# Loading x as plain partition quarters and turning it on VectorE, in place of DMA transposes, in a dense-Mish-dense kernel

## The chip, the cores and the metric

The kernel runs on one core of a Trainium2 chip. The metric is device time in microseconds of one execution; smaller is better. Engines: TensorE (matmuls, with weight loads listed apart as PEld), VectorE (DVE), ScalarE (ACT), GpSimd (POOL) and SyncE (SP). Two engines issue the DMAs here, SP and ACT; each has a queue of its own.

## The reference

```python
B, S, D, F = 1, 2048, 512, 1792          # all bf16
h   = jnp.einsum("bsd,df->bsf", x, w1) + b1
sp  = jnp.log1p(jnp.exp(-jnp.abs(h))) + jnp.where(h > 0, h, 0)
act = h * jnp.tanh(sp)                   # Mish
out = jnp.einsum("bsf,fd->bsd", act, w2)
```

Two dense layers with a Mish between them: 2048 tokens, 512 inputs, 1792 hidden units, 512 outputs.

## The kernel before

The program is written by hand, with one instruction stream for each engine and semaphores between them. Each stream counts its own finished work, and `wait` puts a wait into a stream only where that count isn't known to be reached yet. `load` issues a DMA and gives it a semaphore of its own.

**Layouts.** The first product contracts over D = 512, which is four K tiles of 128 on the partitions. So it needs x with D on the partitions: `xT[p, k, token]`. `w1_sb[p, k, f]` holds w1 with the same split of D. The product comes out as h with 128 hidden units on the partitions and 512 tokens in one PSUM bank (`mm1_step`); ScalarE adds b1 and applies Mish into `a_sb` (`mish`); the second product (`mm2`) contracts over the 14 hidden tiles and gives 128 tokens by 512 outputs, which VectorE copies to `o_sb` and SP stores (`put`).

**Blocks.** The tokens are worked in four blocks of 512. For each block: 14 hidden tiles f, each with four matmuls over K and one Mish; then four token tiles, each with 14 matmuls. Hidden tiles 0 to 3 of block 0 use PSUM banks 0 to 3; all others of the first product use bank 4 + f % 4, so f = 8 waits until the Mish of f = 4 has emptied bank 4. The second product uses banks 0 to 3.

**How x gets transposed.** A token tile is 128 tokens. Tiles 0 and 1 are loaded as they are into `x_nat` and transposed by TensorE against an identity, four pieces of 128x128 each, into PSUM, from where VectorE copies them to `xT` (`transpose_x`). Tiles 2 and 3 come by one DMA transpose straight into `xT`, and so do the blocks 1, 2 and 3, with one DMA transpose each (`load_xT`).

**The start.** Two ordered queues carry the loads. ACT: w1 for f 0 to 3 in two halves (K tiles 0 and 1, then 2 and 3), then b1, then the load of the activation table. SP: x tiles 0 and 1, the DMA transpose of tiles 2 and 3, w1 for f 4 to 7, w1 for f 8 to 13, w2 in two parts, then the DMA transposes of blocks 1 to 3. TensorE first runs ten dummy matmuls on constants (`WARM`, `GAP`), with the transposes of tile 0 between them. Then it works on f 0 to 3 of block 0 in the order in which x comes in: K tiles 0 and 1 on tile 0 (with tile 1's transposes in between), K tiles 0 and 1 on tile 1, K tiles 2 and 3 on both, and last all four K tiles on tiles 2 and 3, one f after the other, each followed by its Mish:

```python
for f in range(F0):
    for k in range(KT):
        mm = mm1_step(0, f, k, f, 2, 4)
    mish(0, f, f, pe.mark(mm))
```

b1 is loaded in 14 rows, copied into a zeroed 32x128 tile, turned by four 32x32 VectorE transposes and cast to float32 (`b1_sb`); every Mish needs it.

Of the kernel before, what the change touches and what calls it, by code (L numbers as in the profile page):

```python
# [4 lines left out]

P = 128
WARM = (512,) * 5 + (128,) * 3
GAP = (128,) * 2
FIRST = ((0, 2), (2, 4))
BLOCKS = (512, 512, 512, 512)  # L10


# [21 lines left out]
def bass_standalone__dense_activation_mish__prompt_kernel(  # L34
# [22 lines left out]
    with ExitStack() as es:  # L57
        def sb(name, shape, t):
            return es.enter_context(nc.sbuf_tensor(name, shape, t))

        x_nat = sb("x_nat", [P, 2, D], BF)
        xT = sb("xT", [P, KT, S], BF)
        w1_sb = sb("w1_sb", [P, KT, F], BF)
        w2_sb = sb("w2_sb", [P, FT, D], BF)
        b1_nat = sb("b1_nat", [FT, P], BF)
# [18 lines left out]
        def load(q, dst, src, name, transpose=False):  # L84
            s = sem(name)
            (q.eng.dma_start_transpose if transpose else q.eng.dma_start)(dst, src).then_inc(s, 16)  # L86
            return (s, 16)

        t_xn, t_w1, t_w2, t_xT = [None] * 2, {}, {}, {}

        def load_x(j):
            t_xn[j] = load(sp, x_nat[:, j, :], x2[j * P:(j + 1) * P, :], "s_xn%d" % j)
# [12 lines left out]
        def load_xT(lo, hi):  # L105
            t = load(sp, xT[:, :, lo:hi], x2[lo:hi, :], "s_xT%d" % lo, True)
            for j in range(lo // P, hi // P):
                t_xT[j] = t

        for ks in FIRST:  # L110
            load_w1(act, slice(*ks), 0, F0)
        load_x(0)
        load_x(1)
        t_b1 = load(act, b1_nat[:, :], b1.rearrange("(j p) -> j p", p=P), "s_b1")
        load_xT(2 * P, 4 * P)
        load_w1(sp, slice(0, KT), 4, 8)
        load_w1(sp, slice(0, KT), 8, FT)
        load_w2(0, 5)
        load_w2(5, FT)
        for s in range(1, len(BLOCKS)):  # L120
            load_xT(starts[s], starts[s + 1])

        t_bz = dve.mark(nc.vector.memset(b1_pad[:, :], 0.0))  # L123
# [9 lines left out]
        def dummy(n):  # L133
            nc.tensor.matmul(ps[:, 7, 0:n], c_w, c_m[:, 0:n], start=True, stop=True)  # L134

        free = [[] for _ in range(8)]
        t_cp = {}
        t_mish = {}


        def transpose_x(j, bank, ks):
            pe.wait(t_xn[j], t_id, *free[bank])
            psb = ps[:, bank, 0:2 * P].bitcast(BF)
            for i, k in enumerate(ks):
                mm = nc.tensor.transpose(psb[:, i * P:(i + 1) * P], x_nat[:, j, k * P:(k + 1) * P], ident[:, :])  # L145
            n = len(ks)
            dve.wait(pe.mark(mm))
            t = dve.mark(nc.vector.tensor_copy(xT[:, ks[0]:ks[0] + n, j * P:(j + 1) * P],  # L148
                                               psb[:, 0:n * P].rearrange("p (k t) -> p k t", k=n)))
            for k in ks:  # L150
                t_cp[j, k] = t
            free[bank] = [t]

        def mm1_step(s, f, k, bank, j0=0, j1=None):
            j1 = BLOCKS[s] // P if j1 is None else j1
            lo, hi = j0 * P, j1 * P
            first = k == 0 and j0 == 0
            if first:
                pe.wait(*free[bank])
            pe.wait(t_w1[k, f])  # L160
            for j in range(starts[s] // P + j0, starts[s] // P + j1):
                pe.wait(t_cp[j, k] if j < 2 else t_xT[j])
            return nc.tensor.matmul(ps[:, bank, lo:hi], w1_sb[:, k, f * P:(f + 1) * P],  # L163
                                    xT[:, k, starts[s] + lo:starts[s] + hi], start=first,
                                    stop=(k == KT - 1 and hi == BLOCKS[s]))

        def mish(s, f, bank, t_mm):
            act.wait(t_b1c, t_mm)
            t = act.mark(act.eng.activation(a_sb[:, f, starts[s]:starts[s + 1]], ps[:, bank, 0:BLOCKS[s]], ACT.Mish,  # L169
                                            bias=b1_sb[:, f:f + 1]))  # L170
            t_mish[s, f] = t
            free[bank] = [t]
# [13 lines left out]
        def mm2(i, lo, hi, bank, q=sp):  # L186
            s = max(b for b in range(len(BLOCKS)) if starts[b] <= i * P)
            pe.wait(*free[bank])
            for f in range(FT):
                pe.wait(t_w2[f], t_mish[s, f])  # L190
                mm = nc.tensor.matmul(ps[:, bank, 0:hi - lo], a_sb[:, f, i * P:(i + 1) * P], w2_sb[:, f, lo:hi],  # L191
                                      start=(f == 0), stop=(f == FT - 1))
# [9 lines left out]
        for k in range(2):  # L202
            for f in range(F0):
                mm1_step(0, f, k, f, 0, 1)
            if k == 0:
                transpose_x(1, 6, (0, 1))
                transpose_x(1, 4, (2, 3))
        dve.wait(t_b1, t_bz)
        t_b1p = dve.mark(nc.vector.tensor_copy(b1_pad[0:FT, :], b1_nat[:, :]))  # L209
        dve.wait(t_b1p)  # L210
        for c in range(P // 32):
            t_b1t = dve.mark(nc.vector.transpose(b1_t[c * 32:(c + 1) * 32, :], b1_pad[:, c * 32:(c + 1) * 32]))  # L212
        dve.wait(t_b1t)
        t_b1c = dve.mark(nc.vector.tensor_copy(b1_sb[:, :], b1_t[:, 0:FT]))  # L214
        for k in range(2):
            for f in range(F0):
                mm1_step(0, f, k, f, 1, 2)
        for k in range(2, KT):
            for f in range(F0):
                mm1_step(0, f, k, f, 0, 2)  # L220
        for f in range(F0):
            for k in range(KT):
                mm = mm1_step(0, f, k, f, 2, 4)
            mish(0, f, f, pe.mark(mm))
# [41 lines left out]
```

## Time and profile before

| | |
|---|---|
| median of three runs | 105.49 us (104.65, 105.49, 105.63) |
| profiled execution | 106.46 us, of which the span from first to last instruction is 105.2 us |
| TensorE busy | 101.3 us |
| ScalarE busy | 39.3 us |
| VectorE busy | 13.6 us |
| DMA | 7.94 MB in 13489 packets |

The profile shows one execution. Its times count from the start of the span. It lists, for each engine, groups of instructions by line of the kernel, operation and tile, with count, busy time and mean duration; the idle time ahead of a group with what ended it; the DMA issues with their time to landing; and the chain of work that ended last, followed back from the last instruction. Matmuls are pipelined and their ends are modelled, so their starts say more than their durations. All engine rows of `load` carry line 86, all matmuls of the first product line 163, of the second line 191; Mish is line 169, the copy of an output line 180.

### The profile page before, as it was taken

The page shows a single profiled execution, that of the slowest core. Times are in us where ns is not written, and L with a number is a line of the kernel's source. Part 1 is how long each engine was busy: PE and PEld are TensorE (multiplying, and loading weights), DVE is VectorE, ACT ScalarE, POOL GpSimd, SP SyncE. Part 2 cuts the span into 40 slices and gives each one's busy share as a digit, 9 for nine tenths or more (in the row PEclk, how much of TensorE's full clock was granted, in tenths as well). Part 3 has the DMA queues.
Part 4 walks back from the last instruction along what each step waited for, and adds up shares of the span by engine and source line. Part 5 has one row for each costly group of instructions (what it writes and reads, how often), then busy time and mean ns, then how long its engine had stood idle before and what let it go on. Part 6 is the DMA issues. An engine that isn't in the chain of part 4 may idle for free.

```text
span 105.2 us, 1142 instructions
## 1 busy us (share of the span) xinstructions
PE 101.3 (96%) x495; PEld 48.9 (47%) x504; DVE 13.6 (13%) x28; ACT 39.3 (37%) x57; POOL 0.7 (1%) x6
## 2 busy tenths in 40 slices
PE   6989999999999999999999999999999999999992
PEld 2667444444444444444444444444444444444462
DVE  0250000022220000022211000022112000011223
ACT  0406977200007777400006877600005777700000
POOL 2000000000000000000000000000000000000000
PEclk9999999999999999999999999999999999999999
DMA  2999999891111000001111000001111000001111
GB/s 40 319 109 361 355 349 275 170 229 44 50 50 50 0 0 6 0 0 50 50 50 50 0 0 0 3 6 50 50 50 50 0 0 0 0 0 53 53 50 50
DMA packets 13489, 7.94 MB, mean 76 GB/s; under 512 B 7852, under 2 KB 13484, under 8 KB 13484
## 3 DMA queue, kind: packets, MB, share of 16 engines
q1 hardware_dynamic: 12768, 7.31, 28.1%
q10 hardware_dynamic: 716, 0.56, 1.7%
q8 instruction: 4, 0.07, 0.3%
q14 instruction: 1, 0.01, 0.0%
HBM read 3.94 MB, written 2.10 MB: 57 GB/s over the span
## 4 chain that ended last, share of the span: by engine, by line
PE 90%; DMA 6%; SPq 1%; issue 1%; DVE 0%
PE ps L191 46%; PE ps L163 44%; DMA xT<-in_x_dram 6%; SPq L86 1%; DVE o_sb L180 0%
## 5 line engine op out<-in xcount | busy, mean ns | idle before, releaser
L169 ACT ACTIVATE a_sb<-ps,b_sb 128x512 bf16<-128x512 f32 x56 | 38.0, 688 | 50.0 <-PE ps L163 50.0
L163 PE MATMUL ps<-xT,w_sb 128*128 128x512 bf16 (+2 forms) x243 | 50.1, 365 | 0.9 <-DMA xT<-in_x_dram 0.6
L191 PE MATMUL ps<-w_sb,a_sb 128*128 128x512 bf16 (+2 forms) x234 | 48.8, 366 | 0.2
L163 PEld LDWEIGHTS ps<-xT,w_sb 128*128 128x128 bf16 x248 | 24.3, 101 | 25.7 <-DMA xT<-in_x_dram 0.9
L191 PEld LDWEIGHTS ps<-w_sb,a_sb 128*128 128x128 bf16 x238 | 22.8, 98 | 25.9
L180 DVE CAST o_sb<-ps 128x512 bf16<-128x512 f32 (+2 forms) x17 | 11.2, 660 | 84.4 <-PE ps L191 84.4
L134 PE MATMUL ps<-const-bfloat16-1.0 128*128 128x512 bf16 (+1 forms) x10 | 3.0, 467 | 0.8 <-PEq L251 0.8
L134 PEld LDWEIGHTS ps<-const-bfloat16-1.0 128*128 128x128 bf16 x10 | 1.2, 139 | 2.2 <-issue 2.2
L128 ACT ACT_TABLE_LOAD x1 | 1.3, 1283 | 2.6 <-issue 2.6
L148 DVE COPY xT<-ps 128x256 bf16<-128x256 bf16 (+2 forms) x4 | 1.1, 291 | 3.5 <-PE ps L145 3.4
L145 PE MATMUL ps<-ident,x_nat 128*128 128x128 bf16 x8 | 1.2, 310 | 0.0
L145 PEld LDWEIGHTS ps<-ident,x_nat 128*128 128x128 bf16 x8 | 0.7, 133 | 0.4 <-DMA x_nat<-in_x_dram 0.3
L212 DVE STREAM_TRANSPOSE b_t<-b_pad 32x32 bf16<-32x32 bf16 x4 | 0.8, 202 | 0.1
L209 DVE COPY b_pad<-b_nat 14x128 bf16<-14x128 bf16 x1 | 0.2, 182 | 1.1 <-DMA b_nat<-in_b_dram 1.1
L126 POOL TENSOR_SCALAR_AFFINE_SELECT ident<-ones 128x128 bf16<-128x128 bf16 x1 | 0.3, 295 | 0.1
L123 DVE MEMSET b_pad<- 32x64 uint32 x1 | 0.1, 112 | 0.9 <-PEq L251 0.9
L124 POOL MEMSET ones<- 128x128 bf16 x1 | 0.2, 205 | 0.3 <-POOLq L251 0.3
L214 DVE CAST b_sb<-b_t 128x14 f32<-128x14 bf16 x1 | 0.2, 175 | 0.0
L251 POOL MEMSET const-bfloat16-1.0<- 128x1 bf16 x1 | 0.1, 102 | 0.0
L251 POOL MEMSET const-uint8-127<- 128x1 uint8 x1 | 0.1, 102 | 0.0
L251 POOL MEMSET const-float32-0.0<- 128x1 f32 x1 | 0.1, 99 | 0.3 <-issue 0.3
L251 POOL MEMSET const-float32-1.0<- 128x1 f32 x1 | 0.1, 99 | 0.0
## 6 DMA issues: line engine op xcount, KB each, us to landing
out_dram<-o_sb SPq DMA_DIRECT2D x15, 128.0 KB, 1.7
w_sb<-in_w_dram SPq DMA_DIRECT2D x1, 1152.0 KB, 11.9
w_sb<-in_w_dram SPq DMA_DIRECT2D x1, 768.0 KB, 7.9
w_sb<-in_w_dram SPq DMA_DIRECT2D x1, 640.0 KB, 9.0
w_sb<-in_w_dram ACTq DMA_DIRECT2D x2, 256.0 KB, 3.8
w_sb<-in_w_dram SPq DMA_DIRECT2D x1, 512.0 KB, 6.4
x_nat<-in_x_dram SPq DMA_DIRECT2D x2, 128.0 KB, 3.0
out_dram<-o_sb SPq DMA_DIRECT2D x1, 96.0 KB, 1.6
```

Source lines behind the costliest of these rows:

```text
L86: (q.eng.dma_start_transpose if transpose else q.eng.dma_start)(dst, src).then_inc(s, 16)
L126: t_id = pool.mark(pool.eng.affine_select(ident[:, :], ones[:, :], pattern=[[1, P]], compare_op=ALU.is_equal, fill=0.0, base=0, channel_mu ...
L128: act.eng.preload_act_table(ACT.Mish)
L134: nc.tensor.matmul(ps[:, 7, 0:n], c_w, c_m[:, 0:n], start=True, stop=True)
L145: mm = nc.tensor.transpose(psb[:, i * P:(i + 1) * P], x_nat[:, j, k * P:(k + 1) * P], ident[:, :])
L148: t = dve.mark(nc.vector.tensor_copy(xT[:, ks[0]:ks[0] + n, j * P:(j + 1) * P], psb[:, 0:n * P].rearrange("p (k t) -> p k t", k=n)))
L163: return nc.tensor.matmul(ps[:, bank, lo:hi], w1_sb[:, k, f * P:(f + 1) * P], xT[:, k, starts[s] + lo:starts[s] + hi], start=first, stop=( ...
L169: t = act.mark(act.eng.activation(a_sb[:, f, starts[s]:starts[s + 1]], ps[:, bank, 0:BLOCKS[s]], ACT.Mish, bias=b1_sb[:, f:f + 1]))
L180: t = dve.mark(nc.vector.tensor_copy(o_sb[:, i, lo:hi], ps[:, bank, 0:hi - lo]))
L191: mm = nc.tensor.matmul(ps[:, bank, 0:hi - lo], a_sb[:, f, i * P:(i + 1) * P], w2_sb[:, f, lo:hi], start=(f == 0), stop=(f == FT - 1))
L212: t_b1t = dve.mark(nc.vector.transpose(b1_t[c * 32:(c + 1) * 32, :], b1_pad[:, c * 32:(c + 1) * 32]))
L251: nc = _bacc.Bacc("TRN2", target_bir_lowering=False, num_devices=1)
```

## The change

Three things change together.

*x.* Only tile 0 still goes through TensorE. Tiles 1 to 15 are loaded into `x_q` with plain DMAs, by quarters: a quarter a holds columns 128a to 128a + 127 of x, on the 32 partitions 32a to 32a + 31, with token t of a group of 32 tokens on partition 32a + t. Each run of a DMA is 128 elements, 256 bytes. VectorE then turns 32x32 pieces (`turn_x`): one instruction for each K tile, over all 128 partitions, reading every fourth element (a step of 8 bytes) and writing `xT`.

*w1.* Reading every fourth element means that partition p of K tile k holds row 4p + k of D, not row 128k + p. w1's rows are loaded in the same order (`"(p k) f -> p k f"`), and tile 0's transposes read `x_nat` with a step of four too.

*Order.* SP now issues x tile 0, two quarters of tile 1, the second half of w1 for f 0 to 3 (which was on ACT), two quarters of tiles 2 and 3, and then w1 and w2 as before; blocks 1 to 3 follow with four DMAs each. ACT issues the first half of w1, two quarters of tile 1, two of tiles 2 and 3, then b1, straight into the zeroed tile. On VectorE the four turns of tile 1 and the four of tiles 2 and 3 stand ahead of b1's; the four turns of each later block stand ahead of the output copies of the block before it. On TensorE tiles 2 and 3 are now worked with K outermost, so the four Mish come at the end. There is one more short dummy.

The diff, without asserts and shape lines:

```diff
-WARM = (512,) * 5 + (128,) * 3
+Q = 32
+WARM = (512,) * 5 + (128,) * 4
-    w1v = w1.rearrange("(k p) f -> p k f", p=P)
+    w1v = w1.rearrange("(p k) f -> p k f", k=KT)
...
-        x_nat = sb("x_nat", [P, 2, D], BF)
+        x_q = sb("x_q", [P, S // Q, P], BF)
+        x_nat = sb("x_nat", [P, D], BF)
...
+        def load_x(q, a, lo, hi):
+            t = load(q, x_q[a * Q:(a + 1) * Q, lo // Q:hi // Q, :],
+                     x2[lo:hi, a * P:(a + 1) * P].rearrange("(g t) e -> t g e", t=Q), "s_x_%d_%d" % (a, lo))
+            t_x.setdefault(lo, []).append(t)
...
-        for ks in FIRST:
-            load_w1(act, slice(*ks), 0, F0)
-        load_x(0)
-        load_x(1)
-        t_b1 = load(act, b1_nat[:, :], b1.rearrange("(j p) -> j p", p=P), "s_b1")
-        load_xT(2 * P, 4 * P)
+        t_bz = dve.mark(nc.vector.memset(b1_pad[:, :], 0.0))
+        load_w1(act, slice(0, 2), 0, F0)
+        t_xn = load(sp, x_nat[:, :], x2[0:P, :], "s_xn")
+        load_x(sp, 0, P, 2 * P)
+        load_x(act, 2, P, 2 * P)
+        load_x(sp, 1, P, 2 * P)
+        load_x(act, 3, P, 2 * P)
+        load_w1(sp, slice(2, 4), 0, F0)
+        load_x(act, 2, 2 * P, 4 * P)
+        load_x(act, 3, 2 * P, 4 * P)
+        load_x(sp, 0, 2 * P, 4 * P)
+        load_x(sp, 1, 2 * P, 4 * P)
+        act.wait(t_bz)
+        t_b1 = load(act, b1_pad[0:FT, :], b1.rearrange("(j p) -> j p", p=P), "s_b1")
         load_w1(sp, slice(0, KT), 4, 8)
         load_w1(sp, slice(0, KT), 8, FT)
         load_w2(0, 5)
         load_w2(5, FT)
         for s in range(1, len(BLOCKS)):
-            load_xT(starts[s], starts[s + 1])
+            for a in range(4):
+                load_x(sp, a, starts[s], starts[s + 1])
...
+        def turn_x(lo, hi):
+            dve.wait(*t_x[lo])
+            for k in range(KT):
+                src = x_q[:, lo // Q:hi // Q, :].rearrange("p g (j k) -> p g k j", k=KT)[:, :, k, :]
+                dst = xT[:, k, lo:hi].rearrange("p (g t) -> p g t", t=Q)
+                t = dve.mark(nc.vector.transpose(dst, src))
+                for j in range(lo // P, hi // P):
+                    t_cp[j, k] = t
...
-        transpose_x(0, 6, (0,))
-        transpose_x(0, 5, (1, 2, 3))
+        transpose_x(6, (0,))
+        transpose_x(5, (1, 2, 3))
         for n in GAP:
             dummy(n)
...
+        turn_x(P, 2 * P)
+        turn_x(2 * P, 4 * P)
+        dve.wait(t_b1)
         (b1's four transposes and cast)
...
+        for j0, j1, k0, k1 in ((0, 1, 0, 2), (1, 2, 0, 2), (0, 2, 2, 4), (2, 4, 0, 4)):
+            for k in range(k0, k1):
+                for f in range(F0):
+                    mm = mm1_step(0, f, k, f, j0, j1)
+                    if j1 == 4 and k == KT - 1:
+                        mish(0, f, f, pe.mark(mm))
...
                 mish(s, f, 4 + f % 4, pe.mark(mm))
+            if s + 1 < len(BLOCKS):
+                turn_x(starts[s + 1], starts[s + 2])
             for i in range(starts[s] // P, starts[s + 1] // P):
```

More of the change, by code (lines that the diff above doesn't have):

```diff
@@ L138, in bass_standalone__dense_activation_mish__prompt_kernel, with transpose_x @@
         t_mish = {}
-        def transpose_x(j, bank, ks):
-            pe.wait(t_xn[j], t_id, *free[bank])
+        def transpose_x(bank, ks):
+            pe.wait(t_xn, t_id)
+            n = len(ks)
             psb = ps[:, bank, 0:2 * P].bitcast(BF)
             for i, k in enumerate(ks):
-                mm = nc.tensor.transpose(psb[:, i * P:(i + 1) * P], x_nat[:, j, k * P:(k + 1) * P], ident[:, :])
-            n = len(ks)
+                mm = nc.tensor.transpose(psb[:, i * P:(i + 1) * P],
+                                         x_nat[:, :].rearrange("p (j k) -> p k j", k=KT)[:, k, :], ident[:, :])
             dve.wait(pe.mark(mm))
-            t = dve.mark(nc.vector.tensor_copy(xT[:, ks[0]:ks[0] + n, j * P:(j + 1) * P],
+            t = dve.mark(nc.vector.tensor_copy(xT[:, ks[0]:ks[0] + n, 0:P],
                                                psb[:, 0:n * P].rearrange("p (k t) -> p k t", k=n)))
             for k in ks:
-                t_cp[j, k] = t
+                t_cp[0, k] = t
             free[bank] = [t]
+        def turn_x(lo, hi):
[6 more added lines that the diff above has]
+                    t_cp[j, k] = t
         def mm1_step(s, f, k, bank, j0=0, j1=None):
@@ L161, in mm1_step @@
             for j in range(starts[s] // P + j0, starts[s] // P + j1):
-                pe.wait(t_cp[j, k] if j < 2 else t_xT[j])
+                pe.wait(t_cp[j, k])
             return nc.tensor.matmul(ps[:, bank, lo:hi], w1_sb[:, k, f * P:(f + 1) * P],
@@ L197, in bass_standalone__dense_activation_mish__prompt_kernel @@
             dummy(n)
-        transpose_x(0, 6, (0,))
-        transpose_x(0, 5, (1, 2, 3))
+        transpose_x(6, (0,))
+        transpose_x(5, (1, 2, 3))
         for n in GAP:
             dummy(n)
[L202 to L212, printed above, removed]
+        turn_x(P, 2 * P)
+        turn_x(2 * P, 4 * P)
+        dve.wait(t_b1)
+        for c in range(P // Q):
+            t_b1t = dve.mark(nc.vector.transpose(b1_t[c * Q:(c + 1) * Q, :], b1_pad[:, c * Q:(c + 1) * Q]))
         dve.wait(t_b1t)
         t_b1c = dve.mark(nc.vector.tensor_copy(b1_sb[:, :], b1_t[:, 0:FT]))
[L215 to L224, printed above, removed]
+        for j0, j1, k0, k1 in ((0, 1, 0, 2), (1, 2, 0, 2), (0, 2, 2, 4), (2, 4, 0, 4)):
[4 more added lines that the diff above has]
+                        mish(0, f, f, pe.mark(mm))
         for s in range(len(BLOCKS)):
```

15 lines of the change are left out of this document (3 added, 12 removed).

## The prediction

> **What bounds the kernel now.** I read the page's busy shares first, then the chain of work that ended last.
>
> ```profile
> PE 101.3 (96%) x495; PEld 48.9 (47%) x504; DVE 13.6 (13%) x28; ACT 39.3 (37%) x57; POOL 0.7 (1%) x6
> ...
> DMA packets 13489, 7.94 MB, mean 76 GB/s; under 512 B 7852, under 2 KB 13484, under 8 KB 13484
> ```
> ```profile
> 1.72 6.33 DMA xT<-in_x_dram
> 8.05 0.05 issue
> 8.10 1.92 PE ps L163 x16
> 10.02 0.05 issue
> 10.07 8.58 PE ps L163 x39
> ...
> 103.33 0.29 DVE o_sb L180
> ```
>
> The reader is to see that the chain has two parts only. Until 8.05 us it is one transfer, the DMA transpose of x's tiles 2 and 3, issued at 1.72. From 8.10 on it is TensorE without a hole: 16 matmuls of 256 columns, 208 of 512 of the first product, 224 of the second. That is 440 units of 512 columns in 95.2 us, 216 ns a unit. So this kernel ends 95.2 us after tiles 2 and 3 land, plus 1.9 us of tail. A change can win only ahead of 8.1 us; behind it a gain must survive every later gate, and a loss counts only if TensorE has to wait.
>
> The timeline shows what TensorE does ahead of that point.
>
> ```profile
> 0.84 2.61 PE L134 MATMUL ps<-const-bfloat16-1.0 128*128 128x512 bf16 x8 [0.84 <-PEq L251]
> ...
> 1.65 0.15 PEld L134 LDWEIGHTS ps<-const-bfloat16-1.0 128*128 128x128 bf16 x1 [0.28 <-issue]
> ...
> 2.08 0.15 PEld L134 LDWEIGHTS ps<-const-bfloat16-1.0 128*128 128x128 bf16 x1 [0.28 <-issue]
> ...
> 3.49 0.34 PEld L145 LDWEIGHTS ps<-ident,x_nat 128*128 128x128 bf16 x4 [0.31 <-DMA x_nat<-in_x_dram]
> ...
> 4.20 0.34 PEld L163 LDWEIGHTS ps<-xT,w_sb 128*128 128x128 bf16 x4 [0.15 <-DMA w_sb<-in_w_dram]
> ...
> 8.10 10.55 PE L163 MATMUL ps<-xT,w_sb 128*128 128x256 bf16 x55 [0.64 <-DMA xT<-in_x_dram]
> 8.81 3.66 ACT L169 ACTIVATE a_sb<-ps,b_sb 128x512 bf16<-128x512 f32 x6 [4.96 <-PE ps L163]
> 12.64 0.69 ACT L169 ACTIVATE a_sb<-ps,b_sb 128x512 bf16<-128x512 f32 x1 [0.18 <-PE ps L163]
> ```
>
> The 512-column warm-up matmuls start 0.43 us apart (1.65, 2.08), twice the 216 ns of later, though the page grants the full clock in all slices; I go by the spacing and call it half rate. The groups in two windows, 4.2 to 6.3 us and 6.6 to 7.4 us, say when it ends:
>
> ```profile
> L163 PEld LDWEIGHTS ps<-xT,w_sb 128*128 128x128 bf16 x17 | 1.8, 143 | 0.2 <-DMA w_sb<-in_w_dram 0.2
> ```
> ```profile
> L163 PEld LDWEIGHTS ps<-xT,w_sb 128*128 128x128 bf16 x6 | 0.6, 99 | 0.1
> ```
>
> A weight load takes 143 ns in the first and 99 ns in the second, so the rate doubled near 6.5. In the kernel before, this moment is nearly free. Between 4.20 and the wait lie 16 matmuls of 128 columns, 4 transposes and 8 matmuls of 256, 9 units in all; wholly at half rate they would take 3.85 us and end at 8.05, when the transfer lands.
>
> **The change part by part.** *Removed:* the chain's first piece, and what it did to other transfers. By windows of one microsecond (the last two columns are the DMA share and GB/s):
>
> ```profile
> 2.00:3.00 1.00, 1.00 (x4) 0.36 (x3) 0.00 (x0) 0.44 (x1) 0.00 (x0) 1.00 0.78 192
> 3.00:4.00 1.00, 0.95 (x9) 0.69 (x8) 0.18 (x1) 0.84 (x1) 0.00 (x0) 1.00 1.07 369
> 6.00:7.00 1.00, 1.00 (x11) 0.89 (x10) 0.31 (x2) 0.00 (x0) 0.00 (x0) 1.00 1.35 88
> 7.00:8.00 1.00, 0.46 (x5) 0.17 (x2) 0.85 (x5) 0.00 (x0) 0.00 (x0) 1.00 0.66 126
> 8.00:9.00 1.00, 0.90 (x9) 0.82 (x10) 0.00 (x0) 0.19 (x1) 0.00 (x0) 1.00 1.13 357
> 17.00:18.00 1.00, 1.00 (x6) 0.47 (x5) 0.00 (x0) 0.82 (x2) 0.00 (x0) 1.00 1.32 302
> ```
>
> Around the first DMA transpose the engines moved 88 and 126 GB/s from 6 to 8 us, against 357 just after. Plain loads in its place should leave no such hole.
>
> *Loads of x.* Tile 1 comes as four quarters of 32 KB in rows of 256 bytes; tiles 2 and 3 as four of 64 KB; later blocks as four of 128 KB.
>
> ```profile
> w_sb<-in_w_dram ACTq DMA_DIRECT2D x2, 256.0 KB, 3.8
> w_sb<-in_w_dram SPq DMA_DIRECT2D x1, 512.0 KB, 6.4
> ```
> ```profile
> DMA to landing us min/median/max: 2.6/3.0/3.3
> ```
> ```profile
> DMA to landing us min/median/max: 3.3/7.2/11.9
> ```
> ```profile
> 0.81 0.87 SPq L86 DMA_DIRECT2D x_nat<-in_x_dram  x2
> ...
> 0.81 0.98 ACTq L86 DMA_DIRECT2D w_sb<-in_w_dram  x2
> ...
> 3.08 3.70 SPq L86 DMA_DIRECT2D w_sb<-in_w_dram  x4
> ```
>
> An issue takes SP 0.44 us and ACT 0.49. (The first landing line is for x_nat, the second for the weights.) The last quarter of tile 1 is the third on ACT, issued at 1.79. It can't land before 1.79 + 2.6 = 4.4, as a tile of x does now. On ACT it stands behind w1's first half, which lands at 0.81 + 3.3 = 4.1, with 64 KB of quarters and the 256 KB of w1's other half from SP beside it: 320 KB at 302 to 369 GB/s is 0.9 to 1.1 us, so 5.1. The late end is the landing of w1's second half now: 3.8 is the median of two and 3.3 the shorter, so 4.3 the longer, and 1.30 + 4.3 = 5.6. I take **5.1**, range 4.4 to 5.8. The window from 17 to 18 us, when the weights are in and the later DMA transposes run, shows 302 GB/s for transfers that the page counts as under 512 bytes (7852 packets), so rows that small need not be slow. [...]
>
> *The VectorE chain.* Its durations:
>
> ```profile
> L180 DVE CAST o_sb<-ps 128x512 bf16<-128x512 f32 x15 | 10.4, 692 | 82.6 <-PE ps L191 82.6
> ...
> L212 DVE STREAM_TRANSPOSE b_t<-b_pad 32x32 bf16<-32x32 bf16 x4 | 0.8, 202 | 0.1
> ...
> L180 DVE CAST o_sb<-ps 128x128 bf16<-128x128 f32 x1 | 0.3, 292 | 0.2 <-PE ps L191 0.2
> ...
> L214 DVE CAST b_sb<-b_t 128x14 f32<-128x14 bf16 x1 | 0.2, 175 | 0.0
> ```
> ```profile
> 6.87 0.90 DVE L212 STREAM_TRANSPOSE b_t<-b_pad 32x32 bf16<-32x32 bf16 x4
> ```
>
> A 32-column transpose takes 202 ns, and four follow each other in 0.90 us, 30 ns between. The casts cost (692 - 292)/384 = 1.04 ns a column. So I estimate 302, 435 and 702 ns for 128, 256 and 512 columns; the bound below is the 202 ns of a single piece, the bound above a full 202 ns for each 32 columns (0.81, 1.62, 3.2 us). I take the slope, because every wide VectorE row follows it. Tile 1: 5.15 + 4 x 0.33 = 6.5, its first quarter of K at 5.45. Tiles 2 and 3: 4 x 0.465, until 8.35. Then b1, now queued behind both: 4 x 0.233 and the cast, until **9.5**; now it was done at 8.0.
>
> *TensorE.* It starts at 4.20 as now: the row there shows it waiting for w1, and the fourth short dummy and the strided read of x_nat lie ahead under that wait (0.15 us of cover; at worst the four weight loads of tile 0 double, 0.6 us, half of it under the gap named next). Tile 0's 8 small matmuls end at 5.06; a gap until 5.5; tile 1's 8 end at 6.36; with the rate doubling at 6.5, the 8 of 256 columns end at 7.3 and the 16 for tiles 2 and 3 at 9.05, the last K quarter being ready at 8.4. Now this point is 8.10 + 16 x 0.109 = 9.85. So TensorE is 0.8 us ahead there. The weights of f 4 to 7 must then be in by 9.05. Now they land at 3.08 + 6.4 = 9.5. In the new order six SP issues stand ahead (3.45), and 1.57 MB in all must move (x's first four tiles and w1's f 0 to 7): 0.19 MB by 3.0, the rest at 300 to 360 GB/s until 6.9 to 7.6, with landing about 8. That holds by a microsecond, if the hole above goes.
>
> *What is late next.* Mish waits for b1 until 9.5, not 8.0. ACT now does six in 3.66 us, (3.66 - 0.69)/5 = 0.59 apart. From 9.55 the fifth starts at 11.9, ends at 12.6, and only then is PSUM bank 4 free for f = 8. TensorE would like it at 9.05 + 4 x 0.866 = 12.5. So f = 8 starts at 12.67, now at 9.85 + 3.46 = 13.31: **0.64 us gained**, and by the 12.64 row ACT's surplus then grows 0.18 us a step, so nothing waits again.
>
> *At no cost:* the 12 transposes of blocks 1 to 3 (2.9 us a block). They lie in VectorE's idle time, 82.6 us of waiting before the casts. Uncovered, block 1's would delay the first cast of an output by 2.9 us, but that has four banks ahead of it. w1's permuted rows keep 1 KB runs, and the second product's weights are called for only at 18.
>
> Sum: 106.46 (profiled, span 105.2 and 1.26 around it) - 0.64 = 105.8; the median of the runs is 0.97 below the profiled one, so **104.85 us**. The runs shown differ by 1%, which is what a measurement of this kernel can tell from no change.
>
> **The rivals.**
> *Tile 1 early, faster than 1%.* With the last quarter in by 4.6 there is no gap; b1 is done at 9.0, TensorE ends the first four at 8.8, and f = 8 starts at 12.2: gain 1.1, 104.4. Speaks for it: the quarters are small; against: three issues in line. If the rate doubles earlier in some runs the gap is all that is left, so 104.1.
> *Nothing won.* Each 0.1 us by which tile 1 lands later passes whole through VectorE, b1, Mish and bank 4. At 5.75 the gain is gone: 105.5. The same if the DMA hole had another cause: then f 4 to 7 land at 9.9.
> *Slower: the gap prolongs half rate.* The rate doubled 5.7 us after TensorE's first work at 0.84, and 3.0 us after it resumed at 3.49 from a break of 0.31 us that may itself have put it off. If the new gap of 0.45 us does that again, the rate doubles between 5.5 + 3.0 and 5.5 + 5.7. From 5.5 there are 14 units; doubling at 8.5 ends them at 10.0, at 11.2 at 11.4, and in the middle (9.85: 10.1 units pass at 0.43 us, 3.9 at 0.216) at 10.7, against 9.85 now: +0.85, 106.3, within 105.6 to 107.0. It decides once the gap exceeds today's break of 0.31 us. Against: of the 3.0 us up to 6.5, TensorE would still work for 85%. [...]
> *Transposes not pipelined.* At the bound above, VectorE's chain lasts 6.5 us longer, and bank 4 comes near 19: 111. No row shows a wide transpose; the casts speak against it.
>
> **How the numbers follow.** Forecast 0.37, early tile 0.25, nothing won 0.21, prolonged half rate 0.12, unpipelined 0.05. Faster by over 1% takes the early case and the forecast's edge: 0.27. Slower takes the last and two thirds of the half-rate case: 0.13. Within 1%: 0.60. The range leaves out the slow tail and little of the early one: 104.0 to 106.4, from the early case's lower end to just past the half-rate case's middle price.
>
> **What would show it.** Right: no idle time of TensorE on a transfer of x near 8 us; VectorE transposes of 128x128, 128x256 and 128x512 near 300, 435 and 700 ns; an idle gap of TensorE on VectorE near 5.1 to 5.5; first Mish near 9.5 and waiting for b1's cast; f = 8 waiting for Mish. Wrong: quarters landing after 5.8, weight loads of 143 ns after 7 us, w1's f 4 to 7 after 9, or transposes that cost by the piece.

## The result and the profile after

The changed kernel takes **108.25 us** (107.70 to 108.50, four runs), the kernel before 105.41 beside it: ratio 1.028, 95% interval 1.021 to 1.034. It is slower; 104.85 had been forecast, and the range up to 106.4 doesn't reach it. A second set of runs of the same kernel, below, gave 107.27, ratio 1.016 (1.008 to 1.023). So the loss is about 1.9 to 2.8 us, and by how much it differs between sets is part of the finding. Medians here are of all executions; the ratios leave out those over 1.5% above the fastest of their kernel.

The profiled execution took 108.5 us, span 107.2. In the rows of the changed kernel the first product is line 180, the second 208, VectorE's turn 167, Mish 186 and the copy of an output 197; the experiments shift these by a few lines. Its page, busy shares and DMA packets:

```profile
PE 102.3 (95%) x501; PEld 48.6 (45%) x501; DVE 22.4 (21%) x45; ACT 38.9 (36%) x57; POOL 0.7 (1%) x6
...
DMA packets 14050, 7.94 MB, mean 74 GB/s; under 512 B 8541, under 2 KB 14045, under 8 KB 14045
```

VectorE has 9 us more to do, as planned. The chain of work that ended last (start, us, what) still has two parts:

```profile
3.17 5.42 DMA x_q<-in_x_dram
8.59 0.03 issue
8.62 0.05 DVEq L26
8.66 0.05 issue
8.71 0.46 DVE xT L167
9.17 0.05 issue
9.22 11.48 PE ps L180 x56
```

Where the DMA transpose of tiles 2 and 3 stood, there is now the last of their four quarters, landing at 8.59, and one VectorE turn. From 9.22 on TensorE works without a hole to the end, so neither b1, nor Mish, nor a PSUM bank, nor w1's later tiles, nor the turns of blocks 1 to 3 hold it up. The loss is made ahead of 9.22 and, as the windows will show, in the two microseconds behind it. The timeline (start, duration; in brackets the idle time ahead of the group and what ended it):

```profile
4.17 0.67 PE L180 MATMUL ps<-xT,w_sb 128*128 128x128 bf16 x8
4.93 0.89 DVE L167 STREAM_TRANSPOSE xT<-x_q 128x128 bf16<-128x128 bf16 x4 [0.55 <-DMA x_q<-in_x_dram]
5.30 0.62 PE L180 MATMUL ps<-xT,w_sb 128*128 128x128 bf16 x8 [0.46 <-DVE xT L167]
7.37 1.58 PE L180 MATMUL ps<-xT,w_sb 128*128 128x256 bf16 x8 [1.45 <-DMA w_sb<-in_w_dram]
8.71 1.42 DVE L167 STREAM_TRANSPOSE xT<-x_q 128x256 bf16<-128x256 bf16 x4 [2.89 <-DMA x_q<-in_x_dram]
9.22 7.16 PE L180 MATMUL ps<-xT,w_sb 128*128 128x256 bf16 x36 [0.27 <-DVE xT L167]
11.83 4.73 ACT L186 ACTIVATE a_sb<-ps,b_sb 128x512 bf16<-128x512 f32 x8 [6.53 <-PE ps L180]
```

Tile 1 is turned from 4.93 on and TensorE has it at 5.30, as forecast. Then come two waits that no step of the prediction had: 1.45 us for w1's second half, which now stands on SP behind x, and then tiles 2 and 3, whose quarters keep VectorE waiting 2.89 us. Windows of the same trace (the last three columns: granted clock of TensorE, DMA share, GB/s):

```profile
4.00:5.00 1.00, 0.84 (x10) 0.50 (x8) 0.43 (x2) 0.98 (x1) 0.00 (x0) 1.00 0.78 143
5.00:6.00 1.00, 0.62 (x8) 0.45 (x8) 0.82 (x4) 0.31 (x1) 0.00 (x0) 1.00 1.05 241
6.00:7.00 1.00, 0.00 (x0) 0.00 (x0) 0.00 (x0) 0.00 (x0) 0.00 (x0) 1.00 1.05 267
```
```profile
4.31:7.72 3.41, 1.50 (x20) 1.12 (x19) 0.96 (x5) 1.00 (x1) 0.00 (x0) 1.00 0.99 236
7.72:11.14 3.42, 3.15 (x17) 1.93 (x15) 2.29 (x9) 0.00 (x0) 0.00 (x0) 0.50 1.05 353
```

The engines moved 143 GB/s from 4 to 5 us and then about 250. After a stretch of 3.41 us in which TensorE was busy for 1.50, the next one of 3.42 us runs at a granted clock of 0.50.

**The kernel before once more.** The first profile of before was of an execution longer than the kernel's usual one (106.46 against a median of 105.4). A second profile, of an execution of 105.27 us (span 104.0), has no transfer in its chain at all:

```profile
5.15 3.53 PE ps L163 x36
8.69 0.20 issue
8.88 8.58 PE ps L163 x39
```
```profile
5.00:6.00 1.00, 1.00 (x15) 0.99 (x13) 0.67 (x4) 0.00 (x0) 0.00 (x0) 1.00 1.26 253
6.00:7.00 1.00, 1.00 (x13) 0.89 (x11) 0.87 (x5) 0.00 (x0) 0.00 (x0) 1.00 1.00 258
7.00:8.00 1.00, 1.00 (x12) 0.90 (x10) 0.11 (x1) 0.52 (x1) 0.00 (x0) 1.00 1.10 361
```

The DMA transpose landed at 6.59, not 8.05, ahead of TensorE's call for it: the 16 matmuls of 256 columns end at 8.69 and take 0.109 each, so they begin at 6.95. Where the first profile had 88 and 126 GB/s, this one has 258 and 361. So the wait that the change removes is no part of the usual run, as far as this one trace near the median shows. Against it, the changed kernel's tiles 2 and 3 start 9.22 - 6.95 = 2.27 us later, and from 9.22 to 11.14 at half clock it loses half of 1.92: 2.27 + 0.96 = 3.2 us, which is the difference of the spans, 107.2 - 104.0.

### The profile page after: what moved, and what is told of

It is laid out like the page before. It is cut to its first block, busy times and chain, and to the rows that moved or that the text cites. A ratio compares the mean times of both kernels' runs of the same rounds, so it can differ in the third digit from the quotient of the medians.

```text
span 107.2 us, 1186 instructions
## 1 busy us (share of the span) xinstructions
PE 102.3 (95%) x501; PEld 48.6 (45%) x501; DVE 22.4 (21%) x45; ACT 38.9 (36%) x57; POOL 0.7 (1%) x6
## 4 chain that ended last, share of the span: by engine, by line
PE 90%; DMA 5%; SPq 2%; DVE 1%; issue 0%; DVEq 0%
PE ps L208 45%; PE ps L180 45%; DMA x_q<-in_x_dram 5%; SPq L86 2%; DVE xT L167 0%; DVE o_sb L197 0%; DVEq L26 0%
## 5 line engine op out<-in xcount | busy, mean ns | idle before, releaser
L180 PE MATMUL ps<-xT,w_sb 128*128 128x512 bf16 (+2 forms) x248 | 51.1, 367 | 2.2 <-DMA w_sb<-in_w_dram 1.4
L167 DVE STREAM_TRANSPOSE xT<-x_q 128x512 bf16<-128x512 bf16 (+2 forms) x20 | 9.8, 546 | 12.8 <-DMA x_q<-in_x_dram 12.8
L140 PE MATMUL ps<-const-bfloat16-1.0 128*128 128x128 bf16 (+1 forms) x11 | 3.1, 452 | 0.8 <-PEq L260 0.8
L155 DVE COPY xT<-ps 128x128 bf16<-128x128 bf16 (+1 forms) x2 | 0.6, 291 | 2.8 <-PE ps L152 2.7
L152 PE MATMUL ps<-ident,x_nat 128*128 128x128 bf16 x4 | 0.6, 311 | 0.0
```

What stands on the lines that cost most here:

```text
L155: t = dve.mark(nc.vector.tensor_copy(xT[:, ks[0]:ks[0] + n, 0:P], psb[:, 0:n * P].rearrange("p (k t) -> p k t", k=n)))
L167: t = dve.mark(nc.vector.transpose(dst, src))
```

## The experiments

Sixteen runs in four sets: e1 to e4 on one chip; and on another e5 to e8, then before again with e9 to e11, then e12 to e14 with the changed kernel again. The runs of one set share the runs of before (medians of 105.3 to 105.4 us).

| run | tile 1 | median, us | ratio (95%) |
|---|---|---|---|
| changed kernel | quarters | 108.25 | 1.028 (1.021 to 1.034) |
| e1 / e2 / e3 / e4 | quarters | 107.64 / 106.49 / 107.17 / 107.39 | 1.017 / 1.011 / 1.016 / 1.019 |
| e5 / e6 | quarters | 107.21 / 107.82 | 1.018 / 1.024 |
| e9 / e11 | quarters | 107.13 / 107.00 | 1.015 / 1.014 |
| e10 (one run) | quarters | 108.16 | none |
| again / e13 | quarters | 107.27 / 107.14 | 1.016 (1.008 to 1.023) / 1.013 (1.006 to 1.021) |
| e7 / e12 / e14 | TensorE | 105.92 / 105.82 / 106.14 | 1.007 (1.003 to 1.010) / 1.005 (1.002 to 1.008) / 1.006 (1.001 to 1.011) |
| e8 | TensorE, DMA transposes | 106.24 | 1.005 (1.000 to 1.009) |

My first theory was the queue: w1's second half moved behind x. The rivals were the short runs of the quarters, w1's permuted rows and the half clock.

**e1: w1's second half back on ACT.**

```diff
         load_w1(act, slice(0, 2), 0, F0)
+        load_w1(act, slice(2, 4), 0, F0)
...
-        load_w1(sp, slice(2, 4), 0, F0)
```

> The changed kernel with w1's second half for f 0 to 3 issued on ACT right behind the first half, as in the kernel before, and not fourth on SP. Theory A (short runs: the 256-byte runs of x cost the DMA engines more than their bytes): the weights land near 5.6 us, as before, but x's quarters of tiles 2 and 3 still land near 8.6, so the gap and the half rate behind it only move: 107.5 to 108.3. Theory B (place in the queue: w1's second half is late only because three x loads stand ahead of it): the weights land near 5.6, TensorE has no gap behind tile 1, the rate isn't halved again, quarters of tiles 2 and 3 by 7.5: 105.3 to 106.2. Theory C (w1's permuted rows are read slowly): the second half still lands near 7.3, and 108.3 stays.

107.64 us (106.41 to 108.49). In the profiled run, its best, the half lands at 5.17 and all quarters by 7.07, but tile 1 now comes last of the first group, at 6.22, and TensorE idles ahead of it:

```profile
6.71 7.57 PE L180 MATMUL ps<-xT,w_sb 128*128 128x128 bf16 x51 [1.60 <-DVE xT L167]
```

With the half on SP it was the half that came late (7.32), with the half on ACT it is tile 1 (6.22, against 4.81): in both of these orders one load is late.

**e2: long runs.** Tiles 1 to 3 in runs of 1 KB, with the same DMAs and bytes.

```diff
-x_q[a*Q:(a+1)*Q, lo//Q:hi//Q, :]  <-  x2[lo:hi, a*P:(a+1)*P]
+x_q[a*Q:(a+1)*Q, ...]             <-  x2[lo + a*Q*m : lo + (a+1)*Q*m, :]
```

> The changed kernel with tiles 1 to 3 of x loaded in runs of 1 KB in place of 256 bytes: the same DMAs, bytes, partitions, queues and order, a quarter of the descriptors (those tiles' values go to other places, so their part of the output is not the reference's). A (short runs): w1's second half lands by 5.8 us, the quarters of tiles 2 and 3 by 6.8, and the time falls to 105 to 106. B (place in the queue): the weights land hardly earlier than 7.0, time 107.5 or more. C (permuted rows of w1): landing times of both stay, 108.3.

106.49 us (106.38 to 106.89), the best of all with tile 1 by quarters, yet w1's second half still landed at 6.94 and the last quarter at 7.33, with 192 GB/s from 4 to 5 us. I first put 1.8 us down to the short runs; the last set (e12, e13, and the changed kernel again at 107.27) doesn't bear that out. All four of these runs do lie below every run of the changed kernel (lowest 107.00), but the two never ran beside each other, so what long runs alone give with w1's half on SP stays open.

**e3: w1's rows unpermuted.**

```diff
-    w1v = w1.rearrange("(p k) f -> p k f", k=KT)
+    w1v = w1.rearrange("(k p) f -> p k f", p=P)
```

> The changed kernel with w1's rows in the order of the kernel before, 128 consecutive rows to a K tile (x is still turned in the permuted order, so the output is not the reference's). C (permuted rows are read slowly): w1's second half lands by 5.8 us instead of 7.3 and the time falls to 105.5 to 106.5. A and B: landings within 0.3 us of the changed kernel, 108.0 to 108.5.

107.17 us (106.87 to 107.35). The low window remains (84 GB/s from 4 to 5 us), w1's second half lands at 6.95, not by 5.8, and the last quarter at 8.13. It is 1.1 below the first set of the changed kernel and 0.1 below the second: no effect that these runs can show.

**e4: dummy matmuls in the gaps.**

```diff
+FILL = {(0, 1): (), (1, 2): (), (0, 2): (512,) * 6, (2, 4): (512,) * 3}
...
+            for n in FILL[j0, j1]:
+                dummy(n)
```

> The changed kernel with six dummy matmuls of 512 columns ahead of K tiles 2 and 3 and three ahead of tiles 2 and 3, so that TensorE works through its gaps. If the second stretch at half rate (7.7 to 11.1 us in the changed kernel) comes from the idle gap, it goes, and with it 0.9 to 1.0 us: 107.3; the landings stay at 7.3 and 8.6. If it comes on its own, the time stays at 108.2 or rises.

107.39 us (107.25 to 107.70); the landings stay (7.01, 8.46) and no run has a half-clock stretch, where three of the changed kernel's first four had one. So the half clock going with the idle time fits, but the changed kernel too has runs without it, and four runs prove little.

**e5: the same 256-byte runs, written over all 128 partitions** instead of 32.

```diff
+t = load(q, x_q[:, lo//Q + a*m : lo//Q + (a+1)*m, :],
+         x2[lo:hi, a*P:(a+1)*P].rearrange("(m p) e -> p m e", p=P), ...)
```

> The changed kernel with tiles 1 to 3 of x read by the same column quarters in the same 256-byte runs, but written over all 128 partitions instead of 32 for each DMA (those tokens' values go to other places, so their part of the output is not the reference's). A1 (the runs are what costs): as the changed kernel, last quarter near 8.3 us, 108.2. A2 (writing to 32 partitions at a time is what costs): as with long runs, last quarter near 7.3, 106.5. D (neither: SP's first read of w1 stalls the queue wherever it stands): w1's second half still lands near 7.0.

107.21 us (106.47 to 107.75): quarters in by 7.20, w1's second half by 6.36, 197 GB/s from 4 to 5 us. With the changed kernel's order of loads the last quarter landed at 8.13 to 8.59 in five other traces (the kernel's own two, e3, e4 and e10), so writing over all partitions did bring it about 1 us earlier; tile 1 came later, at 5.40, and the time didn't follow. The profile shows something else. Weight loads of the first product from 6 to 10.0 us, and from 10.2 on:

```profile
L185 PEld LDWEIGHTS ps<-xT,w_sb 128*128 128x128 bf16 x24 | 3.2, 150 | 0.9
```
```profile
L185 PEld LDWEIGHTS ps<-xT,w_sb 128*128 128x128 bf16 x9 | 0.9, 98 | 0.1
```

By these 150 and 98 ns the start's half rate lasts until 10.1 here. That is the rival "the gap prolongs half rate": TensorE idles 0.74 us ahead of tile 1 in this run, and the rise comes some 3.3 us later than the latest of the other traces (6.8). That the gap put it off is argued from this one trace, and a gap alone doesn't do it: e1 and e13 idle longer at that place (1.60 and 1.28 us), and their weight loads take 98 ns as soon as they go on, at 6.7 and 6.5.

**e6: e1 with dummies** (5 ahead of tile 1, 2 ahead of tiles 2 and 3).

```diff
+FILL = {(0, 1): (), (1, 2): (512,) * 5, (0, 2): (), (2, 4): (512,) * 2}
```

> The changed kernel with w1's second half on ACT and dummy matmuls in the gaps (five of 512 columns ahead of tile 1, two ahead of tiles 2 and 3). With w1's second half on ACT alone the runs spread from 106.4 to 108.5. If that spread is the clock's, the runs come together at 106.0 to 106.6 and all rows stay under 107; if it is the transfers', the spread stays above 1.5 us.

107.82 us (107.49 to 108.30), a miss. The spread of e1 is gone, but a quarter of tiles 2 and 3 landed at 9.36 in the profiled run, and no dummy helps with that.

**e7: the hybrid.** Before's order of loads, tiles 0 and 1 by TensorE, both halves of w1 on ACT, and only tiles 2 and 3 and the later blocks by quarters and VectorE.

```diff
+        load_w1(act, slice(2, 4), 0, F0)
+        t_xn = [load(sp, x_nat[:, j, :], x2[j*P:(j+1)*P, :], ...) for j in range(2)]
+        load_x(act, 2, 2*P, 4*P); load_x(act, 3, 2*P, 4*P)
+        load_x(sp, 0, 2*P, 4*P);  load_x(sp, 1, 2*P, 4*P)
```

> The order of the kernel before (w1's halves on ACT, x tiles 0 and 1 in long runs through TensorE), but tiles 2 and 3 and the blocks by quarters and VectorE, without DMA transposes. If the quarters of tiles 2 and 3 land by 6.5 us, VectorE has the first K tile by 7.0, TensorE doesn't wait there, the rate isn't halved again: 104.5 to 105.0, 0.4 to 0.9 us below the kernel before. If the quarters land after 7.6, no gain: 105.4 or more.

105.92 us (105.65 to 106.93, twelve runs). The quarters land from 6.00 to 6.93 and TensorE waits only for the turn:

```profile
7.52 6.67 PE L176 MATMUL ps<-xT,w_sb 128*128 128x256 bf16 x37 [0.27 <-DVE xT L163]
```

It stays 0.65% behind before (0.33 to 0.97%): landing plus turn reach TensorE at 7.51, where before begins at 6.95.

**e8: before, with w1's second half third on SP.**

```diff
-        for ks in FIRST:
-            load_w1(act, slice(*ks), 0, F0)
+        load_w1(act, slice(*FIRST[0]), 0, F0)
         load_x(0)
         load_x(1)
+        load_w1(sp, slice(*FIRST[1]), 0, F0)
```

> The kernel before with one thing moved: w1's second half third on SP, ahead of the DMA transpose, instead of second on ACT. D (SP's first read of w1 is slow wherever it stands) gives a landing at 6.5 us or later and 106.5 or more. A (the quarter loads around it make it slow) gives 5.2 to 5.8, with the DMA transpose some 0.5 us later: 105.5 to 106.1.

106.24 us over all ten runs; ratio 1.005. In the profiled run (107.79, among its longest) the half landed at 5.73, in time, and TensorE waits 2.18 us for another load, w1 for f 4 to 7, which lands at 11.09. The place on SP alone costs about half a per cent here (0.0 to 0.9), not the 1.6 to 2.8 of the change, and as the whole cause my first theory falls.

**The kernel before again.** No edit.

> The kernel before, unchanged, for a second profile: the first one's span was 105.2 us, the span of most executions near 104.1. If the start makes the difference, tiles 2 and 3 land near 7.0 us here instead of 8.05 and all behind TensorE's first matmul on them takes 95.2 us as before. If it lies elsewhere, they land near 8 again.

105.27 us; its lines stand above.

**e9: long runs and dummies (5 and 2).** The edits of e2 and e4 together.

> The changed kernel with tiles 1 to 3 of x in 1 KB runs (those tokens' part of the output is not the reference's) and dummy matmuls in the gaps. Runs gave 1.76 us, dummies 0.86 us. If they are two costs, the sum gives 105.6 to 105.9. If long runs already spare the second stretch at half rate, the dummies add nothing: 106.3 to 106.6.

107.13 us (106.97 to 109.00): no better than e2 on the other chip, and 0.1 below the changed kernel again. The two gains don't add.

**e10: three shapes off the path.** The start is that of the changed kernel; block 1 comes in 256-byte runs on 32 partitions, block 2 in 256-byte runs on 128, block 3 in 1 KB runs on 32.

```diff
+            if lo == 2 * 512:      # 128 partitions, 256-byte runs
+            elif lo == 3 * 512:    # 32 partitions, 1 KB runs
```

> The cost of the runs by itself, off the path: blocks 1 to 3 are loaded in three shapes, block 1 as in the changed kernel (256-byte runs, 32 partitions a DMA), block 2 with the same runs over 128 partitions, block 3 with 1 KB runs on 32 partitions (blocks 2 and 3 of the output are not the reference's). In the changed kernel such loads ran at 180 to 200 GB/s. A1 (runs): block 2 stays near 190, block 3 reaches 300 or more. A2 (32 partitions): block 2 reaches 250 or more, block 3 stays near 190. The time stays near 108.2.

Block 1's quarters land from 18.5 to 20.8, block 2's to 23.7, block 3's to 25.2. Windows:

```profile
18.00:19.00 1.00, 1.00 (x6) 0.48 (x5) 0.00 (x0) 0.82 (x2) 0.00 (x0) 1.00 1.32 203
20.00:21.00 1.00, 1.00 (x6) 0.48 (x5) 0.09 (x1) 0.82 (x2) 0.00 (x0) 1.00 1.17 204
22.00:23.00 1.00, 0.95 (x5) 0.42 (x5) 1.00 (x3) 0.00 (x0) 0.00 (x0) 1.00 0.86 273
```

With 256-byte runs the busy engines move 203 and 204 GB/s, on 32 partitions or on 128; once the 1 KB runs come in they move 273 at a lower share. So short runs do cost rate here, off the path, and the partitions don't. For the start the second half of this doesn't hold: in e5 the partitions did move the last landing. The time, 108.16 us, with 115 GB/s from 4 to 5 us, is that of the changed kernel.

**e11: all quarters of tiles 2 and 3 on SP.**

```diff
-        load_x(act, 2, 2 * P, 4 * P)
-        load_x(act, 3, 2 * P, 4 * P)
...
+        load_x(sp, 2, 2 * P, 4 * P)
+        load_x(sp, 3, 2 * P, 4 * P)
```

> The changed kernel with the four quarters of tiles 2 and 3 all on SP, behind w1's second half, so that ACT's queue has no x beside it. If it is the quarters on ACT that hold up w1's second half, it lands by 6.2 us instead of 7.0 to 7.3, the last quarter still near 8.5: 107.3 to 107.9. If SP's own queue stalls there, it lands after 6.8: 108.0 to 108.6.

107.00 us (106.54 to 109.52). The low windows stay (154 GB/s from 4 to 5 us, 155 from 6 to 7), so having the quarters of tiles 2 and 3 on two queues is not their cause. Two of tile 1's quarters and w1's first half are on ACT here too.

By then either long runs, or w1 on ACT, or the hybrid seemed to help, each measured against 108.25. The last set took these apart on one chip, with the changed kernel beside them.

**The changed kernel again.** No edit.

> The changed kernel once more, for its spread on the chip of the other runs: 107.6 to 108.5 us. If the half-rate step is what splits its runs, those at a granted clock of 1.0 end 0.4 to 0.9 us ahead of those at 0.984.

107.27 us (107.00 to 107.83), below the 107.6 that had been the low end. Three runs at a granted clock of 1.0 have 107.00, 107.15 and 107.39, the one at 0.984 has 107.83, 0.68 above their middle; in the first set 107.70 was at 1.0 and 108.08 to 108.50 at 0.984. So, within each set, the executions with a half-clock stretch took 0.4 to 0.8 us longer than those without, four of each in all. The profiled run (107.15, span 105.9) is without it:

```profile
5.52 0.65 PE L180 MATMUL ps<-xT,w_sb 128*128 128x128 bf16 x8 [0.18 <-DVE xT L167]
6.80 1.05 PE L180 MATMUL ps<-xT,w_sb 128*128 128x256 bf16 x8 [0.64 <-DMA w_sb<-in_w_dram]
8.30 1.43 DVE L167 STREAM_TRANSPOSE xT<-x_q 128x256 bf16<-128x256 bf16 x4 [2.26 <-DMA x_q<-in_x_dram]
8.80 5.37 PE L180 MATMUL ps<-xT,w_sb 128*128 128x256 bf16 x31 [0.95 <-DVE xT L167]
```

Tiles 2 and 3 start at 8.80, 1.85 later than in the usual run of before, and the spans differ by 1.9. In these two traces that is the whole loss without the half clock.

**e12: the hybrid with long runs** (e7 with e2's edit).

> The hybrid (tiles 0 and 1 turned by TensorE, both halves of w1's first part on ACT, then quarters of tiles 2 and 3), with the quarters of tiles 2 and 3 read in runs of 1 KB; the tokens and columns of these tiles come out in another order, the bytes and DMAs are the same. Short runs as the cause of what is left: the last quarter lands by 6.5 instead of 6.93, the wait of TensorE on VectorE before tiles 2 and 3 goes, first Mish near 9.0, 105.4 us, within 0.2% of before. Order of the loads as the whole cause: landing 6.8 to 7.0 as in the hybrid, 105.9 us.

105.82 us (105.39 to 106.46). The last quarter lands at 6.54, and the chain starts with TensorE itself, as in before:

```profile
5.24 4.11 PE ps L182 x36
9.35 0.05 issue
9.40 8.58 PE ps L182 x39
```

The wait is gone as the short-run theory said; the time is not, only 0.1 below the hybrid. This trace has its rise of the rate at 6.8 instead of 5.5, and these 36 matmuls take 0.6 us longer (4.11 against 3.53); why the median stays 0.5% up isn't settled.

**e13: the changed kernel with w1 on ACT and long runs** (the edits of e1 and e2).

> The changed kernel with w1's second half back on ACT right behind the first and x's tiles 1 to 3 in runs of 1 KB (their tokens and columns come out in another order). Two separate costs: 0.6 us from the first edit and 1.8 from the second add, 105.9 us, w1's second half near 5.2, the last quarter by 6.7. One cause that either edit cures: 106.5 us, as the long runs alone. Tile 1's four DMAs as the cost, whatever their runs: tile 1 lands after 6.0 as with the short runs, TensorE idles more than 1 us ahead of it, 107.0 us or more.

107.14 us (106.97 to 108.83). Neither sum nor single cure: 0.13 below the changed kernel beside it, and the third theory's case, tile 1's own DMAs. w1's second half lands at 5.19, tile 1 only at 5.98:

```profile
6.47 1.51 PE L186 MATMUL ps<-xT,w_sb 128*128 128x128 bf16 x16 [1.28 <-DVE xT L173]
8.53 5.78 PE L186 MATMUL ps<-xT,w_sb 128*128 128x256 bf16 x32 [0.55 <-DVE xT L173]
```

**e14: the hybrid with w1's second half on SP**, where the changed kernel has it.

```diff
-        load_w1(act, slice(2, 4), 0, F0)
         t_xn = [load(sp, x_nat[:, j, :], ...) for j in range(2)]
+        load_w1(sp, slice(2, 4), 0, F0)
```

> The hybrid with w1's second half on SP behind the two tiles of x, where the changed kernel has it, and nothing else. Queue place as the cause as soon as quarters are about: w1's second half lands after 6.5, TensorE waits on it, 107.0 us. Tile 1's four quarters ahead of it as the cause: it lands by 5.8, as in the kernel before with the same place, and the time stays within 0.4 us of the hybrid's 105.9.

106.14 us (105.97 to 107.27); the half landed at 6.35, between the two forecasts, and the time is within 0.4 us of the hybrid's. TensorE waits once, for tiles 2 and 3:

```profile
8.39 5.81 PE L176 MATMUL ps<-xT,w_sb 128*128 128x256 bf16 x33 [0.80 <-DVE xT L163]
```

**What the pairs of the last set say.** Changed kernel and e14 both have w1's second half behind tile 1 on SP, and the same runs, and differ in how tile 1 comes: 107.27 against 106.14. e13 and e12 differ in the same, with w1 on ACT and long runs: 107.14 against 105.82. So tile 1 by four DMAs and VectorE, instead of one DMA, TensorE and a copy, costs 1.1 and 1.3 us, over half of the loss; w1's place and the length of the runs together cost 0.1 with it and 0.3 without. The other 0.5 to 0.8 us stays with all three hybrids, which have tiles 2 and 3 by quarters, b1 behind them and the changed order of the loops; these weren't taken apart. No version beat before.

What the four DMAs do is only partly seen. w1's second half and tiles 2 and 3 land 0.4 us later than in e14 (6.76 and 8.18 against 6.35 and 7.76), but they take no longer from issue to landing: 4.57 us against 4.65 for the half, and for the last quarter, in the changed kernel again and in e14:

```profile
3.17 5.01 DMA x_q<-in_x_dram
```
```profile
2.69 5.07 DMA x_q<-in_x_dram
```

They are issued later, because tile 1 puts two DMAs on SP ahead of them in place of one, and an issue takes SP 0.42 to 0.47 us there. The spans of the two traces differ by the same 0.4 (105.9 and 105.5). The profiled execution of e14 lies 0.6 above its median, so the other 0.7 of the 1.1 us is seen in no trace. In e13 the last quarter is issued 0.93 us later than in e12 and lands 1.41 later (7.95 against 6.54). Also, TensorE has no work between tile 0 and tile 1, where the hybrid has tile 1's transposes. In the changed kernel the engines move 152 and 143 GB/s from 4 to 5 us, 294 in e14; in e13 the low microsecond is the next one, 195 against 292 in e12. Why the engines pause there was not found. By one trace each, the last of tiles 2 and 3 lands at 6.59 in before, 6.93 in e7, 7.76 in e14 and 8.18 in the changed kernel again, so moving w1's half to SP shows more in the landing (0.8 us from e7 to e14) than in the medians (0.2).

## Why the prediction was wrong

**Right.** Tile 1 by quarters: last landing 4.81 and, in the second trace, 5.03 (5.1 taken, range 4.4 to 5.8), TensorE's gap on VectorE from 4.84 to 5.30. The turns of blocks 1 to 3: no cost. w1's permuted rows: none that e3 could show. And VectorE's durations, by the groups of the changed kernel's trace:

```profile
L167 DVE STREAM_TRANSPOSE xT<-x_q 128x512 bf16<-128x512 bf16 x12 | 7.5, 679 | 9.4 <-DMA x_q<-in_x_dram 9.4
L167 DVE STREAM_TRANSPOSE xT<-x_q 128x256 bf16<-128x256 bf16 x4 | 1.4, 413 | 2.9 <-DMA x_q<-in_x_dram 2.9
L167 DVE STREAM_TRANSPOSE xT<-x_q 128x128 bf16<-128x128 bf16 x4 | 0.9, 280 | 0.5 <-DMA x_q<-in_x_dram 0.5
```

280, 413 and 679 ns, where 302, 435 and 702 were estimated; the rival of unpipelined transposes falls. The slope is that of the casts, (679 - 280)/384 = 1.04 ns a column, though not every wide VectorE row has it: the copies of x in the page of before take 225, 291 and 356 ns for 128, 256 and 384 columns, 0.51 ns a column.

**The step that failed** is "Loads of x". It worked out a landing for tile 1's last quarter and for nothing else. The sum then let TensorE run from 6.36 into w1's second half, which the change had moved to SP at 2.18 (it landed at 7.32 and 6.76 in the two traces), and VectorE from tile 1 straight into tiles 2 and 3 (landed at 8.59 and 8.18; the step needed 6.5). So TensorE reached tiles 2 and 3 at 9.22 and 8.80, where the sum has 7.3. Both are moved or added DMAs on the path, and neither had a term; the sign that the prediction had set itself, quarters landing after 5.8, came. Worked with the prediction's own rates (0.19 MB by 3.0 us, the rest of the 1.05 MB due by then at 300 to 360 GB/s), all of it is moved by 5.4 to 5.9: still short of what came by 2 us and more, but a term with a margin of under a microsecond, and a rival of its own. Why these quarters took 4.8 to 5.5 us from issue to landing, where tile 1's took 2.9 to 3.3, stays open.

**"Plain loads should leave no such hole."** They left one, earlier: 143 GB/s from 4 to 5 us instead of 88 and 126 from 6 to 8. And the DMA transpose doesn't always bring the hole: the second trace of before has 258 and 361 GB/s from 6 to 8.

**The median as the profile less 0.97 us.** This took the wait until 8.05 for the usual one. The second trace of before has no wait there, and its f = 4 starts at 8.88, so by the prediction's own step f = 8 starts at 8.88 + 3.46 = 12.34. That is 0.3 us ahead of the 12.67 that was forecast: on this path nothing was to be won, even with no late load. A profile nearly 1 us above the median of its kernel was itself the sign that its path might not be the usual one.

**The rate doubling at 6.5** is no constant of the kernel, either (below). **What is late next**, b1 and bank 4, never decided: b1 was ready at 11.13, and Mish at 11.83 waited for TensorE.

**The slower rival**, a late rise of the rate behind the gap ahead of tile 1, isn't what came in the profiled run: there the rate had risen by 4.31, ahead of the gap (weight loads from 4.31 to 5 take 104 ns). What came, in only some runs, was a second stretch at half clock, behind a stretch with the wait of 1.45 us for w1; that the wait brought it is argued from its place. The rival's price, 0.85 us, stands beside 0.96 in that run and 0.4 to 0.8 between runs, which is luck. Most of the loss is the late start of tiles 2 and 3, for which no rival stood.

**Short rows.** The prediction held that rows of 256 bytes need not be slow, because DMA transposes moved 302 GB/s in packets that the page counts as under 512 bytes. That row said nothing of plain loads: in e10 the engines move 203 and 204 GB/s with runs of 256 bytes, and 273 once the runs of 1 KB come in. The length of the runs isn't what decided the start, though, as e13 shows (107.14 us with runs of 1 KB and w1 on ACT, 107.27 with neither).

## What to carry to other kernels

When loads are reordered, give a landing time to every transfer that the path calls for in the changed part, above all those moved behind others, and count the DMA issues ahead of it on its queue (0.42 to 0.49 us each here); a term that is missing is worse than one that is rough. Before counting a wait as the prize, see whether it is there in a run that takes the median time. And measure a pair of kernels on one chip in one set: between sets this changed kernel alone moved by 1.0 us, enough to make cures out of edits that did little.

## What the runs showed of the hardware

**When the rate doubles is a matter of the execution.** With dummy matmuls from 0.84 us on (in the kernels with tile 1 by quarters one short one more), weight loads of the second trace of before, from 4.6 to 5.45 us and from 5.6 to 6.6, and those of e12 from 5.6 to 6.7 and from 6.9 to 7.9:

```profile
L163 PEld LDWEIGHTS ps<-xT,w_sb 128*128 128x128 bf16 x6 | 0.7, 143 | 0.0
```
```profile
L163 PEld LDWEIGHTS ps<-xT,w_sb 128*128 128x128 bf16 x14 | 1.1, 100 | 0.1
```
```profile
L182 PEld LDWEIGHTS ps<-xT,w_sb 128*128 128x128 bf16 x10 | 1.2, 151 | 0.1
```
```profile
L182 PEld LDWEIGHTS ps<-xT,w_sb 128*128 128x128 bf16 x10 | 1.0, 98 | 0.1
```

The change from about 150 to 98 ns comes at 5.5 and at 6.8; in the other traces it lies between 3.65 (e11, whose two weight loads at 3.74 take 0.15 us together, where e12's at 3.80 take 0.25) and 6.7, except for e5's 10.1. That is a spread of 3.2 us without e5. Each microsecond of it is worth half a microsecond of matmuls as long as TensorE has work, an estimate from the 0.43 us and the 216 ns at which matmuls of 512 columns follow each other ahead of the change and behind it.

**Behind a stretch that was half idle, the half clock came in one trace and not in another.** Three traces show a granted clock of 0.50, each for 3.42 us: from 7.72 to 11.14 in the changed kernel, 7.15 to 10.57 in e10 and 7.06 to 10.48 in e11. That stretch of e11 and the 3.41 us ahead of it, and two stretches of 3.41 us in the changed kernel again (laid from the rise of the weight loads at 5.60, for its clock shows no change):

```profile
3.65:7.06 3.41, 1.86 (x24) 1.33 (x23) 1.42 (x6) 0.65 (x1) 0.00 (x0) 1.00 0.91 203
7.06:10.48 3.42, 3.28 (x17) 2.02 (x16) 2.12 (x9) 0.00 (x0) 0.00 (x0) 0.50 0.98 334
```
```profile
5.60:9.01 3.41, 1.82 (x18) 1.29 (x19) 1.15 (x6) 0.00 (x0) 0.00 (x0) 1.00 1.02 273
9.01:12.42 3.41, 3.36 (x24) 2.26 (x24) 1.58 (x8) 1.67 (x3) 0.00 (x0) 1.00 1.07 373
```

TensorE was busy for 1.86 us of the first and 1.82 of the other, and only the first was followed by a clock of 0.50. So the busy time of such a stretch alone doesn't decide; what does stays open.
